# Gated attention and MLP decode step: the last w2 row in a transfer pair of its own, and the accumulator written out in two 64-row copies and two stores

## The chip, the cores and the metric

The kernel runs on one core of one Trainium2 chip. The metric is the device time of one execution in microseconds, taken as the median of several runs. A separate execution of the same program was recorded by the hardware profiler; rows quoted from "the profile" and "the trace" come from it, and their times count from the start of its span.

## The reference

The step mixes two branches for two tokens (B = 2) of width D = 576. One branch is attention of 32 heads over 4096 cached keys and values of width 128, the other is an MLP of width F = 4608. A gate g per token weighs them.

```python
g = sigmoid((x * gate_w).sum(-1, keepdims=True))
q = (x @ wq) as 32 heads of 128
p = softmax(q . k_cache * Dh ** -0.5)
a = (p @ v_cache, heads joined) @ wo
b = gelu(x @ w1 + b1) @ w2 + b2
out = g * a + (1 - g) * b          # [2, 1, 576], float32
```

Everything is float32. The keys and values alone are 64 pairs (batch, head) of 2 MB each, 268 MB in all, and each byte is used once.

## The kernel before

**Loads.** Nearly all loads are issued by SyncE (SP), in one fixed list named `seq`: first five pieces of wq, five of w1, then keys and values in turn, at last w2 in eight pieces. The function `load()` takes the next entry of the list and issues it. Every piece lands in one of nine buffers of the pool `bp_`, so a load can be issued when an older buffer has been read for the last time. The output weights wo come by `load_wo` through two buffers of their own, one piece for every two heads.

SP's transfers signal on eight semaphores, in turn (DMAHW0 to DMAHW7 in the instruction order below). A transfer is issued only after the one eight places ahead of it on the same semaphore has landed, so at most eight are under way.

**w2.** `load_w2(g, part)` (lines 99 to 104) loads one of eight pieces. A group g holds 1152 rows of w2, nine for each of the 128 partitions. Part 0 has the first five of the nine (2880 numbers for each partition), part 1 the last four (2304 numbers, 9216 bytes). The very last piece is (3, 1). In the trace and in the instruction order these pieces are called `w`, with group and part behind it: w_3_1 is the last.

**The accumulator.** `acc` (line 231) is one PSUM tile. The 576 output columns are cut into NC = 4 segments of DO = 144. Segment s lies in the two partitions 32·s and 32·s + 1, one for each token. `acc_mm` (lines 233 to 237) makes four matmuls, one for each segment, with two columns of weights. The MLP's second bias is the first thing added (line 239), with weights g1, which is 1 - g. Then `wo_mm` adds each head, and at the end of the kernel `mlp_out` (lines 272 to 275) adds the w2 rows, four matmuls for each. In float32 every matmul shows as two records in the trace, so 16 matmuls of w_3_1 are 32 records.

**The end.** After the loop over 64 (batch, head) pairs, lines 397 to 399 run the eight w2 pieces in order. Lines 401 to 404 copy the four segments out of PSUM, two by VectorE (DVE) and two by ScalarE (ACT), each of 2 partitions x 144, into `osb`, a tile of two rows of 576. Line 405 stores it with one transfer issued by SP. The schedule is the order in which the code is written; each engine runs its instructions in that order and waits on semaphores.

Of the kernel before, what the change touches and what calls it, by code (L numbers as in the profile page):

```python
# [8 lines left out]
F32 = mybir.dt.float32  # L9
# [3 lines left out]
P = 128  # L13
# [5 lines left out]
def kernel(  # L19
# [14 lines left out]
    nc = tc.nc  # L34
    B, H, SK, DH = k_cache.shape
    D = x.shape[-1]
# [8 lines left out]
    NG = 4  # L45
# [10 lines left out]
    NC = 4  # L56
    DO = D // NC
    SCALE = float(DH) ** -0.5
    SLOTS = 9
    W2A = 5  # L60

    cp = ctx.enter_context(tc.tile_pool(name="cp", bufs=1))
    bp_ = ctx.enter_context(tc.tile_pool(name="bp_", bufs=SLOTS))
# [4 lines left out]
    ps_acc = ctx.enter_context(tc.tile_pool(name="ps_acc", bufs=1, space=bass.MemoryType.PSUM))  # L68
# [10 lines left out]
    def slot(name, n):  # L79
        return bp_.tile([P, FG * NG], F32, tag="slot", name=name)[:, :n]  # L80
# [18 lines left out]
    def load_w2(g, part):  # L99
        lo, hi = (0, W2A) if part == 0 else (W2A, FR)  # L100
        t = slot(f"w2_{g}_{part}", (hi - lo) * D)
        src = w2[g * FG:(g + 1) * FG].rearrange("(p r) n -> p (r n)", r=FR)
        nc.sync.dma_start(t, src[:, lo * D:hi * D])
        return t.rearrange("p (r n) -> p r n", n=D)

    seq = [("wq", c) for c in range(NX + 1)] + [("w1", c) for c in range(NX + 1)]
# [8 lines left out]
    def load(n=1):  # L115
        for _ in range(n):
            if not seq:
                return
            kind, i = seq.pop()
            if kind == "wq":  # L120
                wqt[i] = load_w(wq, i, "wq")
            elif kind == "w1":
                w1t[i] = load_w(w1, i, "w1_")
            elif kind == "k":
                kt[i] = load_head(k_cache, i, "k")
            elif kind == "v":
                vt[i] = load_head(v_cache, i, "v")
            else:
                w2t[i] = load_w2(*i)
# [8 lines left out]
    b2r = cp.tile([B, D], F32, tag="row", name="b2r")  # L138
# [15 lines left out]
    for j in range(NPB):  # L154
        t = cp.tile([P, 2 * R], F32, name=f"p{j}")
# [15 lines left out]
    for c in range(NX + 2):  # L171
        src = xg[:, c * P:(c + 1) * P] if c < NX else xe[:, c - NX]
# [11 lines left out]
    g1 = cp.tile([P, B], F32, name="g1")  # L184
# [44 lines left out]
        q_unit(0, b)  # L229


    acc = ps_acc.tile([32 * (NC - 1) + B, DO], F32, name="acc")

    def acc_mm(lhsT, rhs, start=False, stop=False):
        for s in range(NC):
            nc.tensor.matmul(  # L236
                acc[32 * s:32 * s + B], lhsT, rhs[:, s * DO:(s + 1) * DO], start=start, stop=stop, skip_group_check=True
            )

    acc_mm(g1[0:1, :], b2r[:1], start=True)  # L240


    hps = [ps_av.tile([P, 512], F32, tag="av", name=f"hps{m}") for m in range(FB - 1)]
# [31 lines left out]
    def mlp_out(g, part, stop=False):  # L275
        lo, hi = (0, W2A) if part == 0 else (W2A, FR)
        for r in range(lo, hi):
            acc_mm(hg[:, g * FR + r], w2t[g, part][:, r - lo], stop=stop and r == hi - 1)
# [73 lines left out]
    def wo_mm(h):  # L352
        acc_mm(oT[h], wot[h // HO][:, h % HO])

    for i in range(N + 3):
# [27 lines left out]
        if k0 < N:  # L383
# [3 lines left out]
            g, r = divmod(k0, UO)  # L387
# [10 lines left out]
        for part in range(2):  # L398
            mlp_out(g, part, stop=(g, part) == (NG - 1, 1))

    osb = cp.tile([B, D], F32, tag="row", name="osb")
    for s in range(NC):
        cpy = nc.vector.tensor_copy if s % 2 == 0 else nc.scalar.copy
        cpy(osb[:, s * DO:(s + 1) * DO], acc[32 * s:32 * s + B])
    nc.sync.dma_start(out.rearrange("b s d -> (b s) d"), osb)


# [26 lines left out]
```

## Time and profile before

| | |
|---|---|
| median of three runs | 734.36 us (734.04 to 735.25) |
| profiled execution, its own time | 735.02 us |
| span of that execution | 733.2 us |
| bytes moved | 309.10 MB, mean 422 GB/s over the span |
| busy share PE, DVE, ACT | 64%, 70%, 43% |
| mean granted TensorE clock | 0.636 |

The span is shorter than the execution's own time by 1.8 us, which lie around it. A busy share is an average over the whole span; what limits the end of the kernel has to be read in a narrow window there. "idle before <-X" in a row means that the engine waited, and that X was the last thing to release it.

### The profile page before, as it was taken

What the parts mean: (1) busy time and instruction counts of PE and PEld (TensorE: products, weight loads), DVE (VectorE), ACT (ScalarE), POOL (GpSimd) and SP (SyncE); (2) the same over time, 40 slices, a digit from 0 to 9 for tenths busy, and PEclk for the clock granted to TensorE, in tenths of its full rate; (3) what the DMA queues carried; (4) which work ended last, traced back from release to release, by engine and by line L of the source; (5) the groups of instructions that cost most, each with busy time, mean ns of one, the idle gap of its engine ahead of it and who ended that gap; (6) DMA issues with size and microseconds to landing.
All of it is one profiled execution on the core that took longest, in us unless ns stands there. A gap on an engine that the chain in (4) does not pass through costs nothing.

```text
span 733.2 us, 8327 instructions
## 1 busy us (share of the span) xinstructions
PE 471.7 (64%) x2728; PEld 222.2 (30%) x2728; DVE 513.8 (70%) x476; ACT 312.3 (43%) x1818; POOL 0.7 (0%) x6
## 2 busy tenths in 40 slices
PE   4660869677755666557575666666576766666676
PEld 2110435344312222223232232232232233323334
DVE  1009869777887778786878868787778877787820
ACT  0104545444554445444455434554445544454410
POOL 0000000000000000000000000000000000000000
PEclk9986666666666665565655655556555655555568
DMA  9999999999999999999999999999999999999994
GB/s 368 427 430 430 433 427 431 427 430 429 430 430 430 426 434 429 429 432 429 430 430 430 428 432 428 429 433 427 432 428 432 426 432 428 431 428 431 429 426 169
DMA packets 25958, 309.10 MB, mean 422 GB/s; under 512 B 3126, under 2 KB 3126, under 8 KB 7228
## 3 DMA queue, kind: packets, MB, share of 16 engines
q1 hardware_dynamic: 25380, 308.56, 98.8%
q8 instruction: 21, 0.34, 0.2%
q14 instruction: 21, 0.17, 0.1%
q10 hardware_dynamic: 536, 0.03, 0.1%
HBM read 308.57 MB, written 0.00 MB: 421 GB/s over the span
## 4 chain that ended last, share of the span: by engine, by line
DMA 85%; PE 10%; DVE 5%; issue 0%; ACTq 0%; DVEq 0%; SPq 0%
DMA k<-in_A_k_cache_dram 76%; PE av L325 8%; DMA w<-in_B_w_dram 6%; DVE k L287 4%; DMA b1T<-in_B_b_dram 3%; PE bp L312 1%; DVE nm L310 0%; DVE s L298 0%; DVE k L294 0%; PE acc L236 0%; PE op L339 0%; ACTq L139 0%; PE op L342 0%; DVEq L429 0%; DVE oT L350 0%
## 5 line engine op out<-in xcount | busy, mean ns | idle before, releaser
L289 ACT ACTIVATE k<-k 128x128 f32<-128x128 f32 x768 | 225.6, 295 | 284.9 <-DVE k L287 284.9
L325 PE MATMUL av<-v,p 128*32 128x512 f32 x1024 | 231.3, 1054 | 0.0
L287 DVE TENSOR_TENSOR k<-k,q 128x1536 f32<-128x1536 f32 x64 | 112.5, 1758 | 166.3 <-DMA k<-in_A_k_cache_dram 166.3
L298 DVE TENSOR_REDUCE s<-k 128x20 f32<-128x2560 f32 x64 | 179.8, 2810 | 0.1
L294 DVE TENSOR_TENSOR k<-k,q 128x2560 f32<-128x2560 f32 x64 | 179.4, 2803 | 0.0
L289 ACT ACTIVATION_READ_ACCUMULATOR k<-k 128x1 f32 x768 | 143.8, 187 | 0.0
L312 PE MATMUL bp<-nm,srow 1*128 1x1 f32 x128 | 36.8, 354 | 134.5 <-DVE nm L310 134.5
L339 PEld LDWEIGHTS op<-sel,avs 128*128 128x128 f32 x512 | 83.2, 247 | 5.2 <-issue 2.7
L339 PE MATMUL op<-sel,avs 128*128 128x1 f32 x512 | 80.7, 279 | 0.7 <-ACT avs L333 0.7
L306 PE MATMUL mt<-ident,m 128*1 128x128 f32 x64 | 20.0, 313 | 85.3 <-DVE m L302 84.7
L312 PEld LDWEIGHTS bp<-nm,srow 1*128 1x128 f32 x128 | 31.3, 302 | 140.1 <-DVE nm L310 138.2
L325 PEld LDWEIGHTS av<-v,p 128*32 128x32 f32 x1024 | 38.1, 159 | 84.5 <-issue 83.5
L333 ACT COPY avs<-av 128x512 f32<-128x512 f32 x64 | 37.5, 586 | 32.4 <-PE av L325 32.3
L306 PEld LDWEIGHTS mt<-ident,m 128*1 128x1 f32 x64 | 5.3, 83 | 141.9 <-DVE m L302 137.9
L236 PE MATMUL acc<-wo,oT 128*2 128x144 f32 x256 | 21.1, 422 | 12.6 <-DMA wo<-in_A_wo_dram 12.0
L342 PE MATMUL op<-rs,ones 128*128 128x1 f32 x128 | 28.7, 294 | 0.0
L219 PE MATMUL qb<-qrow,ident 128*128 128x512 f32 x32 | 26.6, 926 | 0.7 <-ACT q L224 0.7
L342 PEld LDWEIGHTS op<-rs,ones 128*128 128x128 f32 x128 | 26.1, 252 | 0.0
L236 PEld LDWEIGHTS acc<-wo,oT 128*2 128x2 f32 x256 | 6.1, 94 | 60.6 <-issue 50.1
L259 PEld LDWEIGHTS htp<-ident,hrow 128*128 128x128 f32 x72 | 18.4, 331 | 11.5 <-issue 11.2
L224 ACT COPY q<-qb 128x512 f32<-128x512 f32 x16 | 9.4, 586 | 28.9 <-PE qb L219 28.9
L318 ACT ACTIVATE p<-s,bs 128x32 f32<-128x32 f32 x64 | 20.6, 321 | 2.1
(55 smaller groups left out, 172.0 us busy)
## 6 DMA issues: line engine op xcount, KB each, us to landing
k<-in_A_k_cache_dram SPq DMA_DIRECT2D x64, 2048.0 KB, 34.7
v<-in_A_v_cache_dram SPq DMA_DIRECT2D x64, 2048.0 KB, 36.0
w<-in_B_w_dram SPq DMA_DIRECT2D x4, 2304.0 KB, 21.3
wo<-in_A_wo_dram SPq DMA_DIRECT2D x16, 576.0 KB, 36.0
wq<-in_A_wq_dram SPq DMA_DIRECT2D x4, 2048.0 KB, 12.4
w<-in_B_w_dram SPq DMA_DIRECT2D x5, 1152.0 KB, 26.2
w<-in_B_w_dram SPq DMA_DIRECT2D x4, 1440.0 KB, 36.5
wq<-in_A_wq_dram SPq DMA_DIRECT2D x1, 1024.0 KB
```

What stands on the lines that cost most here:

```text
L219: nc.tensor.matmul(ps, ident[:, 32 * j + b:32 * j + b + 1].to_broadcast([P, P]), qrow[:, m * 512:(m + 1) * 512], start=True, stop=True,)
L236: nc.tensor.matmul(acc[32 * s:32 * s + B], lhsT, rhs[:, s * DO:(s + 1) * DO], start=start, stop=stop, skip_group_check=True)
L287: nc.vector.tensor_mul(kt[i][:, :a], kt[i][:, :a], q.to_broadcast([P, a, DH]))
L289: nc.scalar.activation(kt[i][:, r], kt[i][:, r], AF.Copy, accum_out=st[i][:, r:r + 1])
L294: nc.vector.tensor_mul(kt[i][:, a:], kt[i][:, a:], q.to_broadcast([P, R - a, DH]))
L298: nc.vector.tensor_reduce(st[i][:, a:], kt[i][:, a:], AX.X, ALU.add)
L306: nc.tensor.transpose(mt[i], mx[i], ident)
L312: nc.tensor.matmul(bias[i], srow, nm, start=True, stop=True)
L325: nc.tensor.matmul(ps[32 * j:32 * j + 32], p[:, RB * t:RB * t + 32], vt[i][:, RB * t:RB * (t + 1)].rearrange("p r d -> p (r d)"), start=(t ...
L333: nc.scalar.copy(avs[i], ps)
L339: nc.tensor.matmul(ops[i][:, 0:1], avs[i][:, r * DH:(r + 1) * DH], sel[:, r:r + 1], start=(r == 0), stop=(r == RB - 1))
L342: nc.tensor.matmul(ops[i][:, 1:2], ones, rs[i], start=True, stop=True)
```

## The change

The last w2 piece (3, 1) comes in three transfers in place of one: three of its four rows for all 128 partitions, then the fourth row for partitions 0 to 119, then the fourth row for partitions 120 to 127 (`PL = 120`). The destination is the same buffer. The accumulator becomes a tile of 128 partitions, and the bias matmuls use 32 columns of weights, of which 30 are zero, and write all 128 partitions. Two copies of 64 partitions x 144 take it out, the lower half by DVE, the upper by ACT, into a tile `osb` of the same shape. Two stores follow, one for each token: SP stores partitions 0, 32, 64, 96, ACT's queue stores partitions 1, 33, 65, 97.

```diff
+    PL = 120
...
-        nc.sync.dma_start(t, src[:, lo * D:hi * D])
+        if (g, part) == (NG - 1, 1):
+
+            m = hi - 1
+            nc.sync.dma_start(t[:, :(m - lo) * D], src[:, lo * D:m * D])
+            for a, z in ((0, PL), (PL, P)):
+                nc.sync.dma_start(t[a:z, (m - lo) * D:], src[a:z, m * D:hi * D])
+        else:
+            nc.sync.dma_start(t, src[:, lo * D:hi * D])
...
-    acc = ps_acc.tile([32 * (NC - 1) + B, DO], F32, name="acc")
+
+    acc = ps_acc.tile([P, DO], F32, name="acc")
 
     def acc_mm(lhsT, rhs, start=False, stop=False):
+        m = lhsT.shape[-1]
         for s in range(NC):
             nc.tensor.matmul(
-                acc[32 * s:32 * s + B], lhsT, rhs[:, s * DO:(s + 1) * DO], start=start, stop=stop, skip_group_check=True
+                acc[32 * s:32 * s + m], lhsT, rhs[:, s * DO:(s + 1) * DO], start=start, stop=stop, skip_group_check=True
             )
 
-    acc_mm(g1[0:1, :], b2r[:1], start=True)
+    g1z = cp.tile([1, 32], F32, name="g1z")
+    nc.vector.memset(g1z, 0.0)
+    nc.vector.tensor_copy(g1z[:, :B], g1[0:1])
+    acc_mm(g1z, b2r[:1], start=True)
...
-    osb = cp.tile([B, D], F32, tag="row", name="osb")
-    for s in range(NC):
-        cpy = nc.vector.tensor_copy if s % 2 == 0 else nc.scalar.copy
-        cpy(osb[:, s * DO:(s + 1) * DO], acc[32 * s:32 * s + B])
-    nc.sync.dma_start(out.rearrange("b s d -> (b s) d"), osb)
+    osb = cp.tile([P, DO], F32, name="osb")
+    nc.vector.tensor_copy(osb[:P // 2], acc[:P // 2])
+    nc.scalar.copy(osb[P // 2:], acc[P // 2:])
+    for b in range(B):
+        eng = nc.sync if b == 0 else nc.scalar
+        eng.dma_start(out[b].rearrange("o (s n) -> (o s) n", n=DO), osb[b::32])
```

What this makes of the engines' instructions is shown at the end of SP's, TensorE's and ACT's order. In these rows the tile is written ahead of its source, "waits" names the semaphores, the number behind a name is a buffer number, and the code lines after the change are 10 to 14 higher.

The end of SP's order before, from the last piece of group 2 on:

```order
L103 DMA w_2_1_3855<-in_B_w_dram 128x2304 [waits DMAHW3_49,PE_49]
L103 DMA w_3_0_3857<-in_B_w_dram 128x2880 [waits DMAHW4_49,DVE_49,Activation_49]
L103 DMA w_3_1_3889<-in_B_w_dram 128x2304 [waits DMAHW5_49,PE_49]
L405 DMA out_dram<-osb 2x576 [waits DMAHW6_49,DVE_49,Activation_49]
L429 UNCONDITIONAL_BRANCH
```

The same place after the change:

```order
L111 DMA w_2_1_3858<-in_B_w_dram 128x2304 [waits DMAHW3_49,PE_49]
L111 DMA w_3_0_3860<-in_B_w_dram 128x2880 [waits DMAHW4_49,DVE_49,Activation_49]
L107 DMA w_3_1_3892<-in_B_w_dram 128x1728 [waits DMAHW5_49,PE_49]
L109 DMA w_3_1_3892<-in_B_w_dram 120x576 [waits DMAHW6_49]
L109 DMA w_3_1_3892<-in_B_w_dram 8x576 [waits DMAHW7_49]
L419 DMA out_dram<-osb 4x144 [waits DMAHW1_49,Activation_49]
L443 UNCONDITIONAL_BRANCH
```

Two transfers are added behind the first piece of w_3_1; each waits for the transfer eight places ahead of it (the last wo piece on DMAHW6, w_0_1 on DMAHW7). The store has moved to DMAHW1 and no longer waits for DVE by itself.

The end of TensorE's order before, with the matmuls of group 3:

```order
L236 MATMUL acc<-w_3_0_3857,hg 2x144 [waits DMAHW4_49]
L236 MATMUL acc<-w_3_0_3857,hg 2x144 x19
L236 MATMUL acc<-w_3_1_3889,hg 2x144 [waits DMAHW5_49]
L236 MATMUL acc<-w_3_1_3889,hg 2x144 x15
L429 UNCONDITIONAL_BRANCH
```

The same place after the change:

```order
L246 MATMUL acc<-w_3_0_3860,hg 2x144 [waits DMAHW4_49]
L246 MATMUL acc<-w_3_0_3860,hg 2x144 x19
L246 MATMUL acc<-w_3_1_3892,hg 2x144 [waits DMAHW5_49]
L246 MATMUL acc<-w_3_1_3892,hg 2x144 x11
L246 MATMUL acc<-w_3_1_3892,hg 2x144 [waits DMAHW7_49,DMAHW6_49]
L246 MATMUL acc<-w_3_1_3892,hg 2x144 x3
L443 UNCONDITIONAL_BRANCH
```

The first twelve matmuls of w_3_1 wait for the 128-partition transfer alone, the last four for the other two.

The end of ACT's order before:

```order
L333 COPY avs_3851<-av_3842 128x512 [waits PE_49]
L316 COPY bs_3874<-bp_3869 128x1 [waits PE_49]
L318 ACTIVATE p_127,rs_3876<-s_3808,bs_3874 128x32 [waits DVE_49,Activation_49]
L333 COPY avs_3887<-av_3878 128x512 [waits PE_49]
L333 COPY avs_3914<-av_3905 128x512 [waits PE_49]
L404 COPY osb<-acc 2x144 [waits PE_49] x2
L429 UNCONDITIONAL_BRANCH
```

The same place after the change:

```order
L346 COPY avs_3854<-av_3845 128x512 [waits PE_49]
L329 COPY bs_3877<-bp_3872 128x1 [waits PE_49]
L331 ACTIVATE p_127,rs_3879<-s_3811,bs_3877 128x32 [waits DVE_49,Activation_49]
L346 COPY avs_3890<-av_3881 128x512 [waits PE_49]
L346 COPY avs_3919<-av_3910 128x512 [waits PE_49]
L416 COPY osb<-acc 64x144 [waits DVE_49]
L419 DMA out_dram<-osb 4x144 [waits DMAHW0_49,Activation_49]
L443 UNCONDITIONAL_BRANCH
```

ACT's two copies have become one; it waits for DVE, whose last instruction is now the other half's copy (`L415 COPY osb<-acc 64x144 [waits PE_49]`), and a store stands behind it.

## The prediction

> **What bounds the kernel now.** I read the page first, then the chain of waits at the end, then stages of the last 18 us.
>
> ```profile
> DMA  9999999999999999999999999999999999999994
> DMA packets 25958, 309.10 MB, mean 422 GB/s; under 512 B 3126, under 2 KB 3126, under 8 KB 7228
> DMA 85%; PE 10%; DVE 5%; issue 0%; ACTq 0%; DVEq 0%; SPq 0%
> ```
>
> The 16 DMA engines are busy in every slice but the last, and 85% of the chain that ended last is DMA. No part of the change removes bytes (the same 309.10 MB), so only the last slice can become shorter. The chain there, start and length in us:
>
> ```profile
> 705.87 22.37 DMA w<-in_B_w_dram
> 728.24 0.04 issue
> 728.28 2.14 PE acc L236 x32
> 730.42 0.28 DVE osb L404
> ```
>
> The last w2 piece, w_3_1, is issued at 705.87 and lands at 728.24. Then come its 16 matmuls, the copies and the store. Stages of that stretch (window, length, busy time of PE, PEld, DVE, ACT, POOL; granted clock, DMA share, GB/s):
>
> ```profile
> 715.00:718.00 3.00, 2.43 (x69) 2.08 (x72) 0.44 (x2) 0.00 (x0) 0.00 (x0) 1.00 1.00 425
> 718.00:720.00 2.00, 2.00 (x76) 1.72 (x68) 0.00 (x0) 0.00 (x0) 0.00 (x0) 1.00 0.97 410
> 720.00:722.00 2.00, 1.95 (x62) 1.40 (x54) 0.00 (x0) 0.00 (x0) 0.00 (x0) 1.00 0.66 271
> 722.00:724.00 2.00, 1.05 (x36) 0.89 (x39) 0.00 (x0) 0.00 (x0) 0.00 (x0) 1.00 0.36 153
> 724.00:726.00 2.00, 1.05 (x31) 0.62 (x27) 0.00 (x0) 0.00 (x0) 0.00 (x0) 1.00 0.09 34
> 726.00:728.00 2.00, 0.94 (x32) 0.54 (x22) 0.00 (x0) 0.00 (x0) 0.00 (x0) 0.97 0.05 23
> 728.00:730.00 2.00, 1.72 (x32) 0.99 (x32) 0.00 (x0) 0.00 (x0) 0.00 (x0) 0.50 0.00 0
> ```
>
> This is the view that matters. The engines do not finish together: from full share at 718 the DMA share falls to 0.36, 0.09 and 0.05. One engine of sixteen would be 0.06, and one engine's rate is 425/16 = 26.6 GB/s, so from about 724 to 728 **one late DMA engine** works alone while fifteen have nothing left. Its share of w_3_1 ends the load, though all but some 5% of the piece has been there for microseconds. The end of the kernel in detail:
>
> ```profile
> 725.53 1.41 PE L236 MATMUL acc<-w,hg 128*2 128x144 f32 x40 [0.95 <-DMA w<-in_B_w_dram]
> ...
> 728.28 2.10 PE L236 MATMUL acc<-w,hg 128*2 128x144 f32 x32 [1.34 <-DMA w<-in_B_w_dram]
> 730.40 0.63 DVE L404 COPY osb<-acc 2x144 f32<-2x144 f32 x2 [14.31 <-PE acc L236]
> 730.44 0.57 ACT L404 COPY osb<-acc 2x144 f32<-2x144 f32 x2 [16.19 <-PE acc L236]
> 731.09 0.33 SPq L405 DMA_DIRECT2D out_dram<-osb  x1
> ```
>
> The piece before, w_3_0, was complete at 725.5, w_3_1 2.75 us later. That is one engine's eight rows: 8 x 9216 B / 26.6 GB/s = 2.77 us. The late engine thus carries nothing but its own eight partitions.
>
> **The load, split in three.** The first transfer keeps three of four rows, so the late engine's eight partitions shrink to 8 x 6912 B; 8 x 2304 B = 18.4 KB leave it, and 18.4 KB / 26.6 GB/s = **0.69 us**. It lands at about 728.24 - 0.69 = 727.55. This holds for any transfer of 128 rows, whichever engine is late. The two others carry the missing rows, and the last four matmuls wait for them. If the late engine has no part in them, they landed long before. If it has an equal part, eight rows and one of the small transfer, they land 9 x 2304 B / 26.6 GB/s = 0.78 us after the first, at 728.33. TensorE does not get there sooner: it has 12 matmuls, 24 records, from 727.59 on. By the row of 728.28 a record takes 2.10/32 = 66 ns, by that of 725.53 1.41/40 = 35 ns; so 24 of them end between 728.43 and 729.2. Either way the gain at the load is 0.69, and the second and third transfer are hidden behind the first 12 matmuls. Bounds: nothing, if the split does not relieve the late engine, and 0.69.
>
> Their issue: SP issues them behind the first piece, each after the transfer eight places ahead has landed.
>
> ```profile
> 672.37 0.38 SPq L133 DMA_DIRECT2D wo<-in_A_wo_dram  x1
> 678.59 27.60 SPq L103 DMA_DIRECT2D w<-in_B_w_dram  x7
> DMA to landing us min/median/max: 19.1/25.3/36.5
> wo<-in_A_wo_dram SPq DMA_DIRECT2D x16, 576.0 KB, 36.0
> ```
>
> The wo piece, issued at 672.37, lands 36.0 later at 708.4; w_0_1 is issued at 678.59 and lands at most 36.5 later, by 715.1. All engines are full until 718, so both transfers are in line in time: cost 0. If that cover were gone, the delay would first have to use up the 8 to 10 us until the last engine's end. Behind the two waits SP has only the store, at 731.
>
> **The matmuls.** Number and size stay. They start 0.69 earlier, and the granted clock fell from 1.00 to 0.50 at about 727.9 (0.97 mean in 726 to 728). Now about 0.3 us of them lie ahead of that: nine records at 35 ns in place of 66 save 0.28. That drop need not come at the same place in each execution, so I take **0.2**, with bounds 0 (drop before the landing) and 32 x 31 ns = 0.98 (drop after the last matmul).
>
> **The copies.** Before, each engine made two copies, 0.63 us on DVE, side by side with ACT, and the store followed at 731.09, 0.69 after 730.40. Now each makes one; but ACT's waits for DVE, so they stand in a row. A hand-over from DVE to ACT:
>
> ```profile
> 661.31 1.76 DVE L287 TENSOR_TENSOR k<-k,q 128x1536 f32<-128x1536 f32 x1 [1.61 <-DMA k<-in_A_k_cache_dram]
> 663.10 0.31 ACT L289 ACTIVATE k<-k 128x128 f32<-128x128 f32 x1 [4.68 <-DVE k L287]
> L333 ACT COPY avs<-av 128x512 f32<-128x512 f32 x64 | 37.5, 586 | 32.4 <-PE av L325 32.3
> L404 DVE COPY osb<-acc 2x144 f32<-2x144 f32 x2 | 0.6, 298 | 14.3 <-PE acc L236 14.3
> L404 ACT COPY osb<-acc 2x144 f32<-2x144 f32 x2 | 0.5, 272 | 16.2 <-PE acc L236 16.2
> ```
>
> 663.10 - 663.07 is 0.03 us. No row shows 64x144; ACT's copy lies between 272 ns (2x144) and 586 ns (128x512), and I take 272, since it has the same 144 elements for each partition and the rows of 512 add only 0.85 ns per element. So 0.30 + 0.03 + 0.27 and the same 0.06 to 0.08 until the issue: 0.68, against 0.69. **0.0**, with bounds 0 and +0.3.
>
> **The stores.** Two in place of one, on two queues, four rows of 576 B each instead of two of 2304 B. ACT's own issues at the start:
>
> ```profile
> 0.73 0.53 ACTq L139 DMA_DIRECT2D xg<-in_A_x_dram  x1
> 1.30 0.23 ACTq L140 DMA_DIRECT2D xg<-in_gate_w_dram  x1
> ```
>
> 0.23 to 0.53 us against SP's 0.33, so between -0.1 and +0.2, and one more semaphore for SP to look at before the program closes. I take **+0.1**, with bounds -0.1 and +0.4.
>
> **The start.** Two small DVE instructions are added for the 32-column weights.
>
> ```profile
> 11.17 0.17 DVE L188 TENSOR_SCALAR g<-gb 128x2 f32<-128x2 f32 x1
> 31.71 0.42 PE L236 MATMUL acc<-b2r,g 1*2 1x144 f32 x8
> DVE k L287 <- DMA k<-in_A_k_cache_dram: 44.9, 1, 44.9
> ```
>
> DVE has g1 at 11.3 and then waits 44.9 us for keys; TensorE needs the weights at 31.7. Two instructions of 0.2 us are hidden by those 20 us: 0.
>
> **Sum.** -0.69 - 0.2 + 0.0 + 0.1 = -0.8 us. The profiled execution would go from 735.02 to 734.2. It lies 0.66 above the median of the runs, 734.36, which gives **733.6**. A measurement of this kernel can tell about 0.2%, 1.5 us, from no change; -0.8 is 0.11%, so I forecast "same".
>
> [...]
>
> **Rivals.**
>
> *The clock stays full through the last matmuls.* Nothing in the rows ties its fall to the landing, and the earlier they start, the likelier. The sum is -0.69 - 0.98 + 0.1 = -1.6: 732.8, just beyond the border of "faster". Against it: the fall came after four stages in which TensorE waited for DMA, and these stay.
>
> *The split relieves nothing.* The late engine could be late in time, not in bytes: held by something that ends at 728 whatever it carries. Then -0.0 + 0.1: 734.5. Against it speaks that 2.75 us between the last two pieces are just its bytes.
>
> *Slower: 120 rows fall on few engines.* The nearest rows are the counts of packets and of transfers; of the transfers, the first row and the last five are
>
> ```profile
> k<-in_A_k_cache_dram SPq DMA_DIRECT2D x64, 2048.0 KB, 34.7
> ...
> b1T<-in_B_b_dram ACTq DMA_DIRECT2D x1, 18.0 KB, 22.4
> xg<-in_A_x_dram ACTq DMA_DIRECT2D x1, 4.5 KB
> xg<-in_gate_w_dram ACTq DMA_DIRECT2D x1, 2.2 KB
> b2r<-in_B_b_dram ACTq DMA_DIRECT2D x1, 2.2 KB
> out_dram<-osb SPq DMA_DIRECT2D x1, 4.5 KB
> ```
>
> Packets under 512 B are 3126. The eight rows of SP's loads add up to 162 loads of 128 rows; 162 x 16 completions, 16 for b1's load, 2 + 1 + 1 for x, gate_w and b2 and 2 for the store of two rows, with b1's 512 packets of 36 B, make 3126 exactly. So 128 rows use 16 engines, 2 rows two, 1 row one; 120 is not shown. On one engine 120 x 2304 B / 26.6 GB/s = 10.4 us. If that is the late one, the last row lands at 727.55 + 10.4 = 738, then 8 records and the rest: 734.36 + 9.1 = 743.5. On an engine that is free at about 720 it lands near 730 and costs +0.5. It decides from the point at which the row lands after 729.2, about 19 rows beyond the first piece on the late engine. For it: 120 is no multiple of 16. Against it: 120 is a multiple of 15. [...]
>
> **How the numbers follow.** Forecast 0.66 (733.6; with its bounds 732.7 to 734.6), full clock 0.15 (732.8), split without effect 0.13 (734.5), few engines 0.06 (735 to 743). The three runs before lie 1.2 us apart, so a median can miss by half of that. The range of 732.3 to 735.0 holds the first three with this scatter; above it lies the last. Faster than 732.9: half of the full clock and the lower tail of the forecast, 0.18. Slower than 735.8: 0.07, nearly all the last rival. Same: 0.75.
>
> **What would show it.** Right: the last matmuls begin about 0.7 us earlier after the DMA share of one engine; no second gap ahead of the last four; ACT's copy starts at the end of DVE's; under-512 packets 3126 + 15 + 8 + 6 = 3155. Wrong: w_3_1's matmuls still 2.75 us behind the start of w_3_0's, a gap ahead of the last eight records (few engines, or a late small transfer), the two copies side by side, or a store from ACT that lands a microsecond after SP's. A different lag of the late engine, from anything else that the trace does not name, would also break the forecast, in both directions.

## The result, and the profile after

| | before | after |
|---|---|---|
| median | 734.56 us (4 runs) | 743.71 us (743.16 to 744.34, 4 runs) |
| ratio, 95% interval | | 1.0124 (1.0107 to 1.0142) |
| profiled execution, span | 735.02, 733.2 us | 743.87, 742.0 us |

The change makes the kernel 9 us slower. The forecast was 733.6 with a range to 735.0. The rate in 40 slices of the span, first of before, then of after, and the packet counts after (on SP's queue a packet is one row of a transfer, such as 16384 B of keys, or half a row of wo, 2304 B, or a completion of 4 B; before has 16896, 4096 and 2594 of these):

```profile
GB/s 368 427 430 430 433 427 431 427 430 429 430 430 430 426 434 429 429 432 429 430 430 430 428 432 428 429 433 427 432 428 432 426 432 428 431 428 431 429 426 169
GB/s 368 427 427 423 429 424 430 422 430 423 426 427 427 423 430 425 425 426 427 426 426 427 424 427 425 428 427 426 427 426 428 424 427 425 429 422 428 424 422 108
DMA packets 26121, 309.10 MB, mean 417 GB/s; under 512 B 3155, under 2 KB 3163, under 8 KB 7519
```

The 3155 is what the prediction counted for 15 and 8 engines and two stores of four rows. The bytes are the same, but the rate is lower in 37 of the 40 slices, not at the end alone. The stages from 20 to 680 us (columns as in the prediction: window, length, busy PE, PEld, DVE, ACT, POOL, granted clock, DMA share, GB/s), first of before, then of after:

```profile
20.00:680.00 660.00, 424.06 (x2237) 196.21 (x2229) 492.70 (x433) 299.24 (x1753) 0.00 (x0) 0.62 1.01 430
```

```profile
20.00:680.00 660.00, 418.69 (x2223) 201.48 (x2215) 485.47 (x428) 294.29 (x1725) 0.00 (x0) 0.62 1.01 426
```

430 GB/s became 426, at a DMA share of 1.01 in both. SP's timeline of after shows where that leaves the end (start, length):

```profile
713.81 0.33 SPq L107 DMA_DIRECT2D w<-in_B_w_dram  x1
714.68 3.06 SPq L109 DMA_DIRECT2D w<-in_B_w_dram  x2
```

The first of the three new transfers is issued at 713.81; before, the piece was issued at 705.87. **7.9 us are lost before the first instruction at the end that the diff changes.** The rest of the timeline after:

```profile
734.32 4.19 PE L246 MATMUL acc<-w,hg 128*2 128x144 f32 x72 [2.30 <-DMA w<-in_B_w_dram]
736.44 1.55 PEld L246 LDWEIGHTS acc<-w,hg 128*2 128x2 f32 x32 [0.62 <-DMA w<-in_B_w_dram]
738.59 0.30 DVE L415 COPY osb<-acc 64x144 f32<-64x144 f32 x1 [17.80 <-PE acc L246]
738.92 0.27 ACT L416 COPY osb<-acc 64x144 f32<-64x144 f32 x1 [19.98 <-DVE osb L415]
739.22 0.62 SPq L419 DMA_DIRECT2D out_dram<-osb  x1
739.23 0.62 ACTq L419 DMA_DIRECT2D out_dram<-osb  x1
```

The matmuls of w_3_1 start at 736.44 (728.28 before). The two copies stand one behind the other, as the order said. Each store takes 0.62 us to issue instead of 0.33, and from the first store's start to the end of the span it is 742.0 - 739.22 = 2.8 us (733.2 - 731.09 = 2.1 before).

### The profile page after: what moved, and what is told of

Read it like the earlier page. It is cut to its first block, busy times and chain, and to the rows that moved or that the text cites. A ratio compares the mean times of both kernels' runs of the same rounds, so it can differ in the third digit from the quotient of the medians.

```text
span 742.0 us, 8332 instructions
## 1 busy us (share of the span) xinstructions
PE 470.7 (63%) x2728; PEld 228.8 (31%) x2728; DVE 513.7 (69%) x477; ACT 311.7 (42%) x1817; POOL 0.7 (0%) x6
## 2 busy tenths in 40 slices
DMA packets 26121, 309.10 MB, mean 417 GB/s; under 512 B 3155, under 2 KB 3163, under 8 KB 7519
## 4 chain that ended last, share of the span: by engine, by line
DMA 85%; PE 9%; DVE 5%; issue 0%; ACTq 0%; ACT 0%; DVEq 0%; SPq 0%
DMA k<-in_A_k_cache_dram 76%; PE av L338 8%; DMA w<-in_B_w_dram 6%; DVE k L300 4%; DMA b1T<-in_B_b_dram 3%; PE bp L325 1%; DVE nm L323 0%; DVE s L311 0%; DVE k L307 0%; PE acc L246 0%; PE op L352 0%; ACTq L147 0%; PE op L355 0%; PE mt L319 0%; DVE osb L415 0%
## 5 line engine op out<-in xcount | busy, mean ns | idle before, releaser
L338 PE MATMUL av<-v,p 128*32 128x512 f32 x1024 | 226.5, 1035 | 0.0
L352 PEld LDWEIGHTS op<-sel,avs 128*128 128x128 f32 x512 | 87.5, 258 | 3.7 <-issue 2.1
L352 PE MATMUL op<-sel,avs 128*128 128x1 f32 x512 | 84.7, 287 | 0.7 <-ACT avs L346 0.7
L355 PE MATMUL op<-rs,ones 128*128 128x1 f32 x128 | 31.2, 313 | 0.0
L355 PEld LDWEIGHTS op<-rs,ones 128*128 128x128 f32 x128 | 28.9, 278 | 0.0
L246 PE MATMUL acc<-wo,oT 128*2 128x144 f32 x256 | 18.4, 371 | 15.6 <-DMA wo<-in_A_wo_dram 15.0
L227 PE MATMUL qb<-qrow,ident 128*128 128x512 f32 x32 | 23.6, 828 | 0.7 <-ACT q L232 0.7
```

Source lines behind the costliest of these rows:

```text
L227: nc.tensor.matmul(ps, ident[:, 32 * j + b:32 * j + b + 1].to_broadcast([P, P]), qrow[:, m * 512:(m + 1) * 512], start=True, stop=True,)
L246: nc.tensor.matmul(acc[32 * s:32 * s + m], lhsT, rhs[:, s * DO:(s + 1) * DO], start=start, stop=stop, skip_group_check=True)
L338: nc.tensor.matmul(ps[32 * j:32 * j + 32], p[:, RB * t:RB * t + 32], vt[i][:, RB * t:RB * (t + 1)].rearrange("p r d -> p (r d)"), start=(t ...
L352: nc.tensor.matmul(ops[i][:, 0:1], avs[i][:, r * DH:(r + 1) * DH], sel[:, r:r + 1], start=(r == 0), stop=(r == RB - 1))
L355: nc.tensor.matmul(ops[i][:, 1:2], ones, rs[i], start=True, stop=True)
```

## The experiments

**What the theories were.** The change adds two tiles: `g1z` (32 numbers, 128 B for each partition) and an `osb` of its own (144 numbers, 576 B), which before shared the buffer of `b2r`. In the built program the nine load buffers, placed behind these tiles, start at byte 35328 of each partition before, which is 138 x 256, and at 36032 after, which is 140 x 256 + 192. The address theory says that a transfer into a buffer off a multiple of 256 B is slower, all along the kernel. The tail theory says that the transfers, copies and stores at the end cost the 9 us.

### The address alone, and the change without it

Kernel e1 is the kernel before with 704 B of unused tile ahead of the load buffers; e3 and e4 have 64 B and 128 B there. e2 is the changed kernel with 320 B, which brings the buffers back to a multiple of 512 B.

```diff
+    pad = cp.tile([P, 176], F32, name="pad")       # e1; e2: 80, e3: 16, e4: 32
+    nc.vector.memset(pad, 0.0)
     bp_ = ctx.enter_context(tc.tile_pool(name="bp_", bufs=SLOTS))
```

> The kernel before with one unused tile of 704 B per partition ahead of the load buffers, which moves all buffers of the loads by the 128 + 576 B that the change's two new tiles add, and nothing else of the change. Address theory (each packet into a buffer that does not start on a multiple of 256 B takes some ns longer, in all 162 loads): 742 to 744 us, the last w2 piece issued near 714 us, DMA rate in the middle near 426 GB/s. Tail theory (the three transfers, the copies or the stores at the end cost the 9 us): 734.5 us, as before.

> The changed kernel with an unused tile of 320 B per partition ahead of the load buffers, so that these start at a multiple of 512 B again. Address theory: 733.5 to 735 us, the last piece issued near 706 us, first of its three transfers landed about 0.7 us earlier than the 728.2 of before. Tail theory: 743.7 us, as the changed kernel.

> The kernel before with its load buffers moved by 64 B. [...] If any start off a multiple of 256 B costs one step: 742 to 744 us. If only multiples of 64 B matter: 734.5 us. Tail theory: 734.5 us.

> The kernel before with its load buffers moved by 128 B. Cost growing with the distance past a multiple of 256 B: about two thirds of the loss at 192 B, 740 to 741 us. One step for any start off a multiple of 256 B: 742 to 744 us. Only multiples of 64 or 128 B matter, or tail theory: 734.5 us.

| kernel | load buffers past a multiple of 256 B | median | ratio to before, 95% |
|---|---|---|---|
| before, same chip | 0 | 734.31 | |
| e1, before moved | 192 B | 742.01 | 1.0099 (1.0082 to 1.0116) |
| e3, before moved | 64 B | 742.02 | 1.0103 (1.0088 to 1.0118) |
| e4, before moved | 128 B | 742.43 | 1.0104 (1.0089 to 1.0119) |
| e2, changed, moved back | 0 | 735.22 | 1.0010 (1.0001 to 1.0019) |

An unused tile alone costs 7.7 us, and moving the changed kernel's buffers back takes 8.5 us from it. The tail theory falls for all but about 1 us. The loss does not grow from 64 to 192 B (742.02 in e3, 742.01 in e1), so the cost is a step. The middle of e1, as after:

```profile
20.00:680.00 660.00, 414.80 (x2223) 196.92 (x2215) 485.37 (x428) 294.54 (x1725) 0.00 (x0) 0.63 1.01 426
```

The records of single packets in the traces say the same: a packet of 16384 B takes 612.6 ns on average before and in e2, 616.8 ns in e1, e3 and after. With 1056 of them on each engine (16896 in all), 4.2 ns make 4.4 us. The size of a packet hardly matters: from before to e1 those of 2304 B take 3.5 ns longer, those of 18432 B 3.9. All packets together take 5.8 us longer for each engine on average, where the last matmuls start 8.0 us later (736.30 against 728.28); the rest lies in no packet's time. What in the chip costs these nanoseconds no run shows.

### Which buffers pay

g2 leaves the load buffers and moves all that lies behind them by 64 B. g3 makes each of the nine buffers 64 B longer, so that three of nine start on a multiple of 256 B. f3 is the changed kernel with 64 B of unused tile, where the buffers start on an odd multiple of 256 B.

```diff
+    gap = ctx.enter_context(tc.tile_pool(name="gap", bufs=1))       # g2, behind bp_
+    nc.vector.memset(gap.tile([P, 16], F32, name="pad"), 0.0)
...
-        return bp_.tile([P, FG * NG], F32, tag="slot", name=name)[:, :n]
+        return bp_.tile([P, FG * NG + 16], F32, tag="slot", name=name)[:, :n]       # g3
...
+    pad = cp.tile([P, 16], F32, name="pad")       # f3, on top of the change
+    nc.vector.memset(pad, 0.0)
```

> The kernel before with 64 B of unused tile behind the nine load buffers, so that these stay on a multiple of 512 B and everything behind them (the two wo buffers, q, scores, copies of attention results) moves by 64 B. If the loads' destination is what costs: only the 16 wo transfers are touched, 6% of the packets under 2 KB or over, below 1 us: 734.4 to 735.4. If engines that read or write moved tiles cost: near 742.

> The kernel before with 64 B added to each of the nine load buffers, so that they start at 0, 64, 128, 192, 256, 320, 384, 448 and 512 B past a multiple of 512: three of nine on a multiple of 256 B, six not. If each transfer into a buffer that is off pays: six ninths of 7.7 us, 739 to 740. If one cause for the whole kernel (the pool's start): 734.4 as before, or 742 in full.

> The changed kernel with 64 B of unused tile ahead of the load buffers, which then start at a multiple of 256 B but not of 512 B. If 256 B decides: as with the multiple of 512 B, 735.2 us. If 512 B decides: 743 to 744 us.

g2: 734.41 against 734.58 (ratio 0.9997, 0.9988 to 1.0006). Engines that read or write moved tiles cost nothing that can be measured; it is the destination of the loads into the nine buffers. g3: 739.04 against 734.58, 4.5 us where six ninths of 7.7 are 5.1: the loss goes about with the number of buffers that are off. Its middle runs at 428 GB/s, between the two:

```profile
20.00:680.00 660.00, 421.01 (x2229) 203.61 (x2225) 488.00 (x430) 295.53 (x1733) 0.00 (x0) 0.61 1.01 428
```

The 16384 B packets of keys and values, taken 128 at a time in order of their start, show the nine buffers in turn: their mean runs from 612.0 to 616.2 ns with a period of nine transfers in g3, and shows no such period before (611.5 to 612.2) or in e1 (615.1 to 616.7). But that each transfer pays for its own buffer alone does not follow. The two wo buffers of g2 are 64 B off, and the 2304 B packets of wo take 93.3 ns there, against 93.2 before and 96.7 in e1, where the load buffers are off as well. A transfer that is off among others that are not paid nothing here; how the transfers under way act on each other was not tried.

f3: 735.23 (ratio 1.0013, 1.0004 to 1.0022), as e2 with 735.22: buffers on an odd multiple of 256 B cost nothing against buffers on a multiple of 512 B.

### The split alone, and another split

With its buffers back in place the changed kernel is still 0.9 us slower than before, where the prediction's sum said 0.8 faster. f1 is the kernel before with the split alone. g1 takes the last row in one transfer of 128 partitions; g4 takes 112 and 16 in place of 120 and 8.

```diff
+            nc.sync.dma_start(t[:, :(m - lo) * D], src[:, lo * D:m * D])
-            for a, z in ((0, PL), (PL, P)):
-                nc.sync.dma_start(t[a:z, (m - lo) * D:], src[a:z, m * D:hi * D])
+            nc.sync.dma_start(t[:, (m - lo) * D:], src[:, m * D:hi * D])       # g1, else as f1
...
+    PL = 112       # g4, else as f1
```

> The kernel before with the last w2 piece in three transfers and nothing else of the change; its load buffers stay where they were. Address theory, with the prediction's step for the load: 0.5 to 1.0 us faster than before, 733.4 to 734.0. If the split itself costs (a small transfer that lands late, the issue of two more transfers): same as before or up to 1 us slower.

> The kernel before with the last w2 piece in two transfers: three rows for all 128 partitions, then the fourth row for all 128. In the split with 120 and 8 partitions the piece ahead of it, w_3_0, was complete 0.7 to 0.8 us later than before (matmuls from 726.3 instead of 725.5). If the 120-partition transfer, which is dealt over the engines in another way than 128, gets in the way of the late engine: here w_3_0 is complete at 725.5 again, the first transfer near 727.6, the second near 728.3, and only its four matmuls come behind: 0.5 to 1.2 us faster than before, 733.2 to 733.9. If any further small transfer does it: w_3_0 at 726.3 and 734.5 to 735.0.

> The split kernel with 112 and 16 partitions in place of 120 and 8, nothing else of the change. [...] If any other dealing gets in the way of the late engine: w_3_0 complete at about 726.3. If only the count of 15 engines does: 725.5.

f1: 734.96 against 734.46 (1.0006, 0.9997 to 1.0015), no gain. g1: **733.44 against 734.58 (0.9986, 0.9977 to 0.9995)**, faster than both kernels. g4, a single execution: 734.49. The ends of f1, g1 and g4, in this order:

```profile
726.34 1.41 PE L244 MATMUL acc<-w,hg 128*2 128x144 f32 x40 [0.30 <-DMA w<-in_B_w_dram]
728.40 1.37 PE L244 MATMUL acc<-w,hg 128*2 128x144 f32 x32 [0.65 <-DMA w<-in_B_w_dram]
729.31 0.14 PEld L244 LDWEIGHTS acc<-w,hg 128*2 128x2 f32 x8 [0.31 <-DMA w<-in_B_w_dram]
```

```profile
725.39 1.41 PE L242 MATMUL acc<-w,hg 128*2 128x144 f32 x40 [2.00 <-DMA w<-in_B_w_dram]
727.46 1.16 PE L242 MATMUL acc<-w,hg 128*2 128x144 f32 x32 [0.67 <-DMA w<-in_B_w_dram]
728.64 0.63 DVE L410 COPY osb<-acc 2x144 f32<-2x144 f32 x2 [14.03 <-PE acc L242]
729.34 0.32 SPq L411 DMA_DIRECT2D out_dram<-osb  x1
```

```profile
726.46 1.41 PE L244 MATMUL acc<-w,hg 128*2 128x144 f32 x40 [0.28 <-DMA w<-in_B_w_dram]
728.54 1.27 PE L244 MATMUL acc<-w,hg 128*2 128x144 f32 x32 [0.67 <-DMA w<-in_B_w_dram]
729.35 0.14 PEld L244 LDWEIGHTS acc<-w,hg 128*2 128x2 f32 x8 [0.22 <-DMA w<-in_B_w_dram]
```

The rows with x40 are w_3_0, a piece that no kernel here changes. It is complete at 725.5 before and at 725.4 in g1, at 726.3 in f1 and 726.5 in g4, though w_3_1 is issued between 705.5 and 705.9 in all four. So the late engine loses 0.8 us or more before it begins with w_3_1, and only where the last row comes as 120 + 8 or 112 + 16. From w_3_0 to the first transfer of w_3_1 it needs 2.06 us in f1 (728.40 - 726.34) against 2.75 before: the 0.69 are there, and are spent already. Stages of f1 and of g1 in the stretch in which the loss comes about:

```profile
720.00:722.00 2.00, 2.00 (x48) 1.29 (x44) 0.00 (x0) 0.00 (x0) 0.00 (x0) 0.61 0.63 237
722.00:724.00 2.00, 2.00 (x72) 1.56 (x68) 0.00 (x0) 0.00 (x0) 0.00 (x0) 1.00 0.42 154
```

```profile
720.00:722.00 2.00, 2.00 (x76) 1.70 (x68) 0.00 (x0) 0.00 (x0) 0.00 (x0) 1.00 0.64 264
722.00:724.00 2.00, 1.38 (x48) 0.92 (x36) 0.00 (x0) 0.00 (x0) 0.00 (x0) 1.00 0.45 181
```

About as many engines are busy, but they move a tenth less: 237 GB/s at a share of 0.63, against 264 at 0.64. In the packet records of 718.5 to 724.5 a packet of 6912 B takes 262 ns on average in g1, 293 in f1 and 295 in g4. It is some packets that take longer, not all: from 712 to 730 us, 55 packets of f1 take over 4% longer than is usual for their size, some of them of pieces ahead of w_3_1. All 55 start between 719.57 and 723.22, while the early engines write the last row (718.94 to 724.59). g4 has 71 such packets; before, f2 and g1 have one each, though g1 writes its last row in the same stretch. So while rows of the 120- or 112-partition transfer are written, other packets are slowed. What slows them no run shows.

### The copies and stores alone

f2 is the changed kernel without the split, its buffers in place; f4 is the kernel before with its store in two.

```diff
-        if (g, part) == (NG - 1, 1):       # f2: the split undone, 320 B of unused tile as in e2
...
+    for b in range(B):                     # f4, in place of the one store
+        eng = nc.sync if b == 0 else nc.scalar
+        eng.dma_start(out[b], osb[b:b + 1])
```

> The changed kernel without the split, with the copies and stores of the change, its load buffers back on a multiple of 512 B. The aligned changed kernel stood 0.9 us above before; if the two stores cost that and the split gains 0.7, this one stands 1.3 to 1.8 us above before, 735.8 to 736.2. If the split is what costs: 734.3.

> The kernel before with its store in two, one token by SP and one by ACT's queue, copies as before. If two queues that issue at the same moment cost (0.62 us for each issue in the changed kernel against 0.33 for the one store before): 0.5 to 0.8 us slower than before, 734.9 to 735.1. If the four short rows of each store cost: within 0.2 us of before.

f2: 734.88 against 734.46 (1.0007, 0.9998 to 1.0016). f4: 734.39 (0.9998, 0.9989 to 1.0008). The end of f2, then of f4:

```profile
728.30 1.16 PE L241 MATMUL acc<-w,hg 128*2 128x144 f32 x32 [1.34 <-DMA w<-in_B_w_dram]
729.53 0.30 DVE L410 COPY osb<-acc 64x144 f32<-64x144 f32 x1 [14.47 <-PE acc L241]
729.87 0.27 ACT L411 COPY osb<-acc 64x144 f32<-64x144 f32 x1 [17.67 <-DVE osb L410]
730.16 0.65 SPq L414 DMA_DIRECT2D out_dram<-osb  x1
730.17 0.62 ACTq L414 DMA_DIRECT2D out_dram<-osb  x1
```

```profile
730.53 0.32 SPq L407 DMA_DIRECT2D out_dram<-osb  x1
730.55 0.25 ACTq L407 DMA_DIRECT2D out_dram<-osb  x1
```

In f2 the store starts 0.63 us after the first copy (0.69 before), and from there to the end of the span (733.0) it is 2.8 us, 0.7 more than before. In f4 two queues issue at the same moment, each in 0.32 us or less, and the rest takes 732.7 - 730.53 = 2.2 us. So the second queue costs next to nothing; it is the stores of four rows of 576 B, 32 partitions apart, that take 0.3 us longer to issue and end 0.7 us later. Whether the number of rows, their size or their distance does it was not tried. f2's median fits neither of the two values that were expected, 735.8 to 736.2 and 734.3. It rises by 0.4 only; the matmuls of f2 ran at full clock to their end in the profiled execution (the row of 728.30: 1.16 us for 32 records, 2.10 before), so the clock can have hidden part of the loss.

## Why the prediction was wrong

**The step that failed** is the one at the top: "No part of the change removes bytes ... so only the last slice can become shorter." It shut off the first 39 slices from gains, and silently from losses too. The added tiles were costed as two DVE instructions in "The start", at 0, and never as bytes that move all load buffers. In this kernel, whose DMA share is 1.01 over the middle, some 4 ns for each packet come to 5.8 us of packet time and to 7.7 us at the end (e1), and no chain of waits or order of instructions shows it; the address of a buffer has to be worked out. By the runs it is the multiple of 256 B that decides (735.23 on an odd one in f3, 742.01 to 742.43 off it in e1, e3 and e4), and the cost does not grow with the distance from it (742.02 at 64 B, 742.01 at 192 B).

**The few-engines rival.** Its 743.5 us lies beside the measured 743.71 by accident, and by a slip: 738 less 728.24, less 24 records of 66 ns that are done by then, plus 0.1, is 8.3 and not 9.1, which gives 742.7. It also had nearly all of the 0.07 that the prediction gave to anything above 735.8. The 15 and the 8 in the count of 3155 had no run behind them when it was made. The run of after shows them: of its 2619 packets of 4 B on SP's queue, 16 for each of 162 loads and 4 for the store leave 23, and the landing records are 15 for the 120 rows and 8 for the 8. And 7.9 us are gone before these transfers are issued.

**The load, -0.69.** The first transfer is shorter by just that, but 120 + 8 takes about 0.8 back on the piece ahead (f1). With 128 rows, g1, w_3_1's matmuls start at 727.46 instead of 728.28: -0.82. The term had the right size for another split. The rival in which the split relieves nothing named f1's outcome (734.5, measured 734.96) but not its reason: the late engine did shed its bytes.

**"TensorE does not get there sooner."** Wrong: in f1 its weight loads stand idle for 0.31 us ahead of the last eight records, and the 32 records take 1.37 us, 0.2 more than in f2 and g1. At full clock 24 records take 0.9 us. By the landing records of f1 the first transfer is complete at 728.36, the other two at 729.03 and 729.21: the late engine has a part in both, and its nine rows come 0.85 us behind, about the 0.78 of the prediction, on top of the 0.8 lost ahead.

**The clock, -0.2.** The place of the fall does vary: the last 32 records take 2.10 us before, 1.16 in f2 and g1, 1.37 with the gap in f1. This alone moves single executions by up to 0.9 us, whatever the change, and it is in all medians here: the 33 executions of before beside f1 and f2 lie in two groups, 17 up to 734.46 and 16 from 734.66 to 735.33, and the median falls on the edge between them. The lowest times suffer least from it: 734.35 for f1 and 734.74 for f2 against 733.96, 733.23 for g1 against 734.00. By them the split costs 0.4, the end 0.8, and the split over 128 rows gains 0.8. The rows at full clock say about the same: the last matmul ends at 729.77 in f1 and 728.62 in g1, against 729.46 in f2, whose load is as before.

**The copies, 0.0.** Right: they stand in a row, and the store starts 0.06 us earlier in f2. ACT's 64x144 takes 0.27 us, as its 2x144 did.

**The stores, +0.1.** Mis-sized: +0.7 against an upper bound of 0.4. The shape of the stores was the reason, not the second queue that the bound was built on.

**The sum without the address**: e2 stands 0.9 us above before (0.1 to 1.4 by the interval), the split 0.5 (f1) and the end 0.4 (f2). Neither of the change's two ideas gains anything, and each alone lies within what its interval allows for no change. The changed kernel stands 1.7 us above e1, where both have moved buffers. The end of e1's profiled execution, of span 740.3, shows what that is made of:

```profile
736.30 1.16 PE L238 MATMUL acc<-w,hg 128*2 128x144 f32 x32 [1.37 <-DMA w<-in_B_w_dram]
737.48 0.63 DVE L406 COPY osb<-acc 2x144 f32<-2x144 f32 x2 [13.61 <-PE acc L238]
738.17 0.33 SPq L407 DMA_DIRECT2D out_dram<-osb  x1
```

Against the rows after the change, the last matmuls start 0.14 us earlier in e1 and take 0.97 less up to the copies, at full clock to their end (a clock of 0.50 in 736 to 738 after the change), and the time from the store to the end of the span is 0.7 shorter. So in these two executions the clock makes over half of the 1.7, and the stores most of the rest; the lowest times of the two kernels, 743.16 and 741.88, are 1.3 apart.

## What to carry to other kernels

Where DMA is full, take a new or resized tile as a change to every load behind it (7.7 to 8.1 us here, e1, e3 and e4): work out the start of the load buffers, and keep it on a multiple of 256 B with the allocation made on purpose. When one late DMA engine ends a kernel, split the last piece along its free dimension over all 128 partitions, so that most of the compute on it begins earlier (g1, 1.1 us by the medians); last rows of 120 + 8 and 112 + 16 partitions slowed the packets around them here (6912 B in 293 and 295 ns, against 262 with 128). A forecast that says where time can be won should ask the same question again for losses.

## What the runs showed of the hardware that was not expected

- Loads into buffers 64, 128 or 192 B past a multiple of 256 B ran at 426 GB/s instead of 430, and a 16384-byte packet took 616.8 ns at 64 B (e3) and at 192 B (e1, after) instead of 612.6; the size of the offset made little difference (742.01 to 742.43 us), and that of the packet too (3.5 ns more at 2304 B, 3.9 at 18432 B, in e1).
- The wo loads of g2, alone 64 B off among load buffers on a multiple of 256 B, kept their packets at 93.3 ns (93.2 before, 96.7 in e1).
- Last-row transfers of 120 + 8 and of 112 + 16 partitions lengthened other engines' 6912-byte packets from 262 to 293 and 295 ns while they ran; a transfer of 128 partitions did not (262).
- A store of four 576-byte rows from partitions 32 apart took 0.62 to 0.65 us to issue, a store of one 2304-byte row 0.25 to 0.32.
